# Weight passes in halves on GpSimd, all upper weight parts on ScalarE, and one-column softmax sums in a Longformer-and-MLP kernel

## The chip, the core and the metric

The kernel runs on one core of a Trainium2 chip. The core has five instruction streams: TensorE (PE, with its weight loads shown as PEld), VectorE (DVE), ScalarE (ACT), GpSimd (POOL) and SyncE (SP), which here issues all DMAs. Each engine takes its instructions strictly in the order in which they stand in its stream. The metric is the device time of one execution in microseconds, and of several runs the median. The profile is one such execution, and its lines are in microseconds unless marked ns.

## The reference

Two stages are computed one after the other. First an attention with a window and with global tokens, for 8 batches and 8 heads of width 64, with 512 local and 32 global tokens:

```python
s_g  = scale * q_g @ k_all^T            # 32 global queries see all 544 keys
s_ll = scale * q_l @ k_l^T              # 512 local queries, |i - j| <= 32 only
s_lg = scale * q_l @ k_g^T              # and the 32 global keys
out  = softmax(...) @ concat(v_g, v_l)
```

Then every token (8 x 544 = 4352 tokens of 512 features) goes through a two-layer network with 2048 hidden units and a slope per unit for negative values:

```python
h = x @ w_in
g = maximum(h, 0) + alpha * minimum(h, 0)
y = g @ w_out
```

Everything is wanted near single precision. The kernel gets there with operands that are split in two: a rounded upper part and the rest, and three matrix products of such parts in place of one.

## The kernel before, in words

**The network** is cut into 9 groups of tokens (8 batches of 512 local tokens, and one group of the 256 global tokens) and 16 blocks of 128 hidden units, so 144 steps. A step has 12 matmuls for the first layer (`f1`: `h_ps` from `xh`, `xl` and the weights `wt`), two VectorE passes for the activation (L407, L408), a rounding on ScalarE (`gh`, L410), a subtraction on GpSimd (`gl`, L411), and two steps later 12 matmuls for the second layer (`f2`: accumulated in `o`).

**The attention** goes by pairs of heads, 32 pairs of four quarter steps each, and runs ahead of the network: 19 steps (`NPRE`) of attention stand before the first network step, and later each network step carries a quarter of a pair. The first five pairs (`NRAW`) take a path with transposes on TensorE, the others go through DRAM. In each quarter step `local_scores` (L246, L250) makes two score tiles with their row minima `mn` and their row sums `z`, and the function that it returns, `softmax_tail`, adds 1e-9 to the two sums (L211), inverts them (L212) and scales the two tiles (L217 on ScalarE, or L215 on GpSimd in two quarter steps of the first pair).

**The weights** arrive in double precision, as pairs of 32-bit words, in 32 pieces of 128 x 512 (16 blocks, two layers). Each piece is turned to single precision and split in two. `decode_words` uses ScalarE twice (L113, L114), VectorE three times (L115, L117, L118, each over 128 x 512) and GpSimd once (L120, an integer addition over 128 x 512). One round later `split_weights` makes the upper part `wt[:, 0]` by a rounding copy, on VectorE for the blocks 0 to 7 (L127; `WV = range(0, 8)`, so 16 pieces) and on ScalarE for the blocks 8 to 15 (L129), and the lower part `wt[:, 1]` on GpSimd (L130). In the first 19 steps 13 pieces are decoded, later 3 pieces in two steps, until none is left; this ends while the first batch is in the network. After that only attention and network remain.

**What sets the order.** The code is written in steps, and a scheduler with a model of the engines then orders the instructions of every engine. From the 25th step on (`PIN`) TensorE's matmuls keep the order of the program; what belongs to the attention gets a higher priority from the fifth step on. Matmuls without use (`warm`, two and two in each of the first 18 steps) only keep TensorE busy.

Tiles of the names `wt`, `wr` and `g` are buffers of 128 x 512 elements in SBUF; `wt` in the first rows of a piece is the tile under work, and in L127 to L130 the final pair of parts.

Of the kernel before, what the change touches and what calls it, by code (L numbers as in the profile page):

```python
# [8 lines left out]
F32 = mybir.dt.float32  # L9
# [4 lines left out]
ALU = mybir.AluOpType  # L14
# [12 lines left out]
NWARM = 18  # L27
WARM = (2, 2)
NRAW = 5
WV = range(0, 8)  # L30
NWB = 33
NST = 18
NNP = [(0, 0), (0, 2)]
# [27 lines left out]
def longformer_ffn(ctx: ExitStack, tc: tile.TileContext, qk, qkr, gn, vt, vx, w, alpha, out):  # L61
    nc = tc.nc
# [35 lines left out]
    def stage(name, dtype=F32):  # L98
        return work.tile([128, 512], dtype, tag="st", name=name, bufs=NST)
# [9 lines left out]
    def decode_words(f, j):  # L109
        words = wraw.pop((f, j)).rearrange("p (n two) -> p n two", two=2)  # L110
        low, high = words[:, :, 0], words[:, :, 1]
        t, r = stage("wt"), stage("wr", I32)
        nc.scalar.activation(t, high.bitcast(F32), AF.Abs)  # L113
        nc.scalar.activation(r, low, AF.Copy, scale=2.0**-29)  # L114
        nc.vector.tensor_scalar(t, t, CLAMP_LO, CLAMP_HI, op0=ALU.max, op1=ALU.min)  # L115
        tu = t.bitcast(U32)
        nc.vector.tensor_scalar(tu, tu, 3, 0x3FFFFFFF, op0=ALU.logical_shift_left, op1=ALU.bitwise_and)  # L117
        nc.vector.scalar_tensor_tensor(tu, high, 0xC0000000, tu, op0=ALU.bitwise_and, op1=ALU.bitwise_or)  # L118
        ti = t.bitcast(I32)
        nc.gpsimd.tensor_tensor(ti, ti, r, op=ALU.add)  # L120
        wmid[f, j] = t

    def split_weights(f, j):
        t = wmid.pop((f, j))
        wt = wpool.tile([128, 2, 512], F32R, tag="w", name="wt")
        if f in WV:
            nc.vector.tensor_copy(wt[:, 0, :], t)  # L127
        else:
            nc.scalar.copy(wt[:, 0, :], t)  # L129
        nc.gpsimd.tensor_tensor(wt[:, 1, :], t, wt[:, 0, :].bitcast(F32), op=ALU.subtract)  # L130
        wts[f, j] = wt

    rmask = stage("rmask")[:, 0:480].rearrange("p (i n) -> p i n", i=3)
# [71 lines left out]
    def small(name, n=2):  # L205
        return work.tile([128, n], F32, tag=name, name=name, bufs=3)

    def softmax_tail(ranges, z, n, pool=False):
        parts = 128
        rz = small("rz")  # L210
        nc.vector.tensor_scalar(rz[:parts, 0:n], z[:parts, 0:n], 1e-9, None, op0=ALU.add)  # L211
        nc.vector.reciprocal(rz[:parts, 0:n], rz[:parts, 0:n])  # L212
        for e, r in enumerate(ranges):
            if pool:
                nc.gpsimd.tensor_scalar(r, r, rz[:parts, e : e + 1], 1.0, op0=ALU.mult, op1=ALU.mult)  # L215
            else:
                nc.scalar.activation(r, r, AF.Copy, scale=rz[:parts, e : e + 1])  # L217

    def local_scores(P, h, a, pool=False):
# [24 lines left out]
        for e, pr in enumerate(ranges):  # L244
# [4 lines left out]
            )  # L249
            nc.scalar.activation(pr, pr, AF.Exp, bias=mn[:, e : e + 1], scale=-1.0, accum_out=z[:, e : e + 1])  # L250
        return lambda: softmax_tail(ranges, z, 2, pool)

    gbank = {}
# [282 lines left out]
    def weights_step(u):  # L536
        k = state[0]
        n = RATE[0][u % len(RATE[0])] if u < NPRE else RATE[1][u % len(RATE[1])]
        new = [i for i in range(k, min(k + n, len(pieces)))]
        for i in new:  # L540
            if i + ahead < len(pieces):
                load_weights(*pieces[i + ahead])
            decode_words(*pieces[i])
        state[0] += len(new)
        done.append([pieces[i] for i in new])
        if len(done) > 1:
            for key in done.pop(0):
                split_weights(*key)
# [10 lines left out]
    for t in range(-NPRE, NT + LAG):  # L559
# [6 lines left out]
        G, f = divmod(t + 1, NF)  # L566
# [93 lines left out]
```

## Time and profile before

| | |
|---|---|
| median of 3 runs | 1049.59 us (1046.12 to 1050.47) |
| the profiled execution | 1047.16 us, of which the span from the first to the last instruction is 1045.4 us |
| PE busy | 989.7 us (95% of the span) |
| DVE busy | 702.2 us (67%) |
| ACT busy | 502.4 us (48%) |
| POOL busy | 429.6 us (41%) |
| mean granted TensorE clock | 0.966 of full speed |

A row of a group names the source line, the engine, the operation, the tiles with their shapes and the count; then the busy time in us and the mean duration of one in ns; then the idle time of the engine just before these instructions, with what ended it. A row of a timeline names the start in us, the duration in us, the engine, the line, the operation and the tiles. A row of a table by stages names the stretch, its length, and then for PE, PEld, DVE, ACT and POOL the busy time and in brackets the number of instructions; last come the granted TensorE clock, the share of time that the DMA engines were busy, and the GB/s that they moved. The granted clock is 1.00 at full speed and 0.50 at half.

### The profile page before, as it was taken

The numbers are of one execution on the slowest core, as the hardware profiler recorded it, in microseconds if no ns is written. First come the engines' busy times: TensorE is split into PE (matmuls) and PEld (weight loads), VectorE is DVE, ScalarE is ACT, GpSimd is POOL, SyncE is SP. The second block draws the span as 40 slices with busy tenths as digits, with TensorE's granted clock in tenths as the row PEclk, the third lists the DMA queues.
The fourth block names the chain that finished last, engine by engine and source line by source line (L and its number), as shares of the span: only waits on it lengthen the run. The fifth ranks groups of instructions, "written<-read, shape, count | busy, mean of one in ns | idle before, by whom it ended". The sixth has DMA issues, their size and how long they took to land.

```text
span 1045.4 us, 16948 instructions
## 1 busy us (share of the span) xinstructions
PE 989.7 (95%) x5466; PEld 795.0 (76%) x5466; DVE 702.2 (67%) x2189; ACT 502.4 (48%) x1337; POOL 429.6 (41%) x342
## 2 busy tenths in 40 slices
PE   7789988789999999999999999999999999999998
PEld 4455666667888878887888788878887788888798
DVE  8984999987666866676667766676667666322322
ACT  5465576655544555465455545555445443211121
POOL 6621777774333334343444344434443431122222
PEclk9985798899999999999999999999999999999999
DMA  9461266435544554455444554455445433100010
GB/s 338 177 204 67 100 208 211 138 89 166 147 142 141 156 170 140 142 163 170 140 145 142 155 159 141 139 162 154 139 141 169 152 116 90 52 1 1 1 41 21
DMA packets 103626, 139.39 MB, mean 133 GB/s; under 512 B 11056, under 2 KB 59952, under 8 KB 103536
## 3 DMA queue, kind: packets, MB, share of 16 engines
q1 hardware_dynamic: 103536, 138.30, 43.2%
q8 instruction: 43, 0.70, 0.3%
q14 instruction: 47, 0.39, 0.1%
HBM read 104.57 MB, written 33.69 MB: 132 GB/s over the span
## 4 chain that ended last, share of the span: by engine, by line
PE 73%; DVE 17%; DMA 3%; issue 3%; ACT 1%; POOL 1%; SPq 1%; DVEq 0%; ACTq 0%; POOLq 0%
PE o L93 31%; PE h_ps L93 29%; PE o_ps L93 5%; PE s_ps L93 4%; PE g_ps L93 3%; DVE wt L118 2%; DVE wt L115 2%; DMA rawq<-in_qk_dram 2%; DVE wt L117 2%; DVE p_sb L246 2%; DVE g L407 1%; DVE pt_sb L300 1%; DVE rz L211 1%; DVE g L408 1%; DMA out_dram<-ost 1%
## 5 line engine op out<-in xcount | busy, mean ns | idle before, releaser
L411 POOL TENSOR_TENSOR gl<-g,gh 128x512 fp32r<-128x512 f32 (+1 forms) x144 | 178.8, 1242 | 441.2 <-ACT gh L410 410.1
L93 PE MATMUL h_ps<-xh,wt 128*128 128x512 f32 (+1 forms) x1152 | 350.2, 387 | 6.9 <-DVE g L408 6.6
L93 PE MATMUL o<-gh,wt 128*128 128x512 f32 (+1 forms) x1152 | 282.1, 387 | 3.5 <-ACT ost L305 3.5
L93 PEld LDWEIGHTS o<-gh,wt 128*128 128x128 f32 x1152 | 204.9, 188 | 52.9 <-ACT ost L305 9.3
L93 PEld LDWEIGHTS h_ps<-xh,wt 128*128 128x128 f32 x1152 | 206.4, 191 | 46.3 <-DVE g L408 4.1
L93 PE MATMUL h_ps<-xl,wt 128*128 128x512 f32 (+1 forms) x576 | 221.6, 386 | 1.1 <-DVE xl L390 1.1
L410 ACT CAST gh<-g 128x512 fp32r<-128x512 f32 (+1 forms) x144 | 85.8, 596 | 270.7 <-DVE g L408 254.2
L407 DVE TENSOR_SCALAR g<-h_ps,alpha_sb 128x512 f32<-128x512 f32 (+1 forms) x144 | 103.1, 716 | 117.0 <-PE h_ps L93 116.1
L217 ACT ACTIVATE p_sb<-p_sb,rz 128x192 f32<-128x192 f32 (+1 forms) x252 | 102.6, 455 | 151.8 <-DVE rz L212 149.7
L93 PE MATMUL o<-gl,wt 128*128 128x512 f32 (+1 forms) x576 | 150.6, 383 | 0.3 <-POOL gl L411 0.3
L250 ACT ACTIVATE p_sb<-p_sb,mn 128x192 f32<-128x192 f32 (+2 forms) x256 | 115.9, 454 | 39.1 <-DVE mn L246 38.8
L93 PEld LDWEIGHTS h_ps<-xl,wt 128*128 128x128 f32 x576 | 109.1, 190 | 25.0 <-DVE xl L390 1.8
L93 PEld LDWEIGHTS o<-gl,wt 128*128 128x128 f32 x576 | 105.0, 188 | 24.4 <-POOL gl L411 0.7
L300 DVE STREAM_TRANSPOSE pt_sb<-sg_sb 32x64 f32<-32x64 f32 x432 | 102.0, 236 | 28.5 <-ACT sg_sb L283 21.6
L196 POOL TENSOR_TENSOR hi<-rawq,hi 64x512 fp32r<-64x512 f32 x54 | 70.6, 1307 | 121.7 <-DMA vt<-in_vt_dram 46.7
L211 DVE TENSOR_SCALAR rz<-z 128x2 f32<-128x2 f32 x128 | 54.7, 427 | 90.3 <-ACT p_sb L250 89.4
L408 DVE SCALAR_TENSOR_TENSOR g<-h_ps,g 128x512 f32<-128x512 f32 (+1 forms) x144 | 93.9, 652 | 2.8
L93 PE MATMUL o_ps<-pt_sb,vt 128*64 128x160 f32 (+4 forms) x808 | 70.4, 309 | 20.2 <-DVE mn L246 18.9
L199 POOL TENSOR_TENSOR kl<-rawk,hi 128x640 fp32r<-128x640 f32 x54 | 86.6, 1603 | 3.8
L93 PEld LDWEIGHTS o_ps<-pt_sb,vt 128*64 128x64 f32 (+2 forms) x808 | 51.9, 146 | 38.6 <-DVE mn L246 23.2
L246 DVE CUSTOM_DVE_ANT_0 p_sb<-s_ps,mask 128x192 f32<-128x192 f32 x216 | 71.9, 362 | 9.4 <-PE s_ps L93 8.2
L327 DVE STREAM_TRANSPOSE p_sb<-p_sb 128x896 f32<-128x896 f32 x54 | 59.6, 1104 | 9.0 <-ACT p_sb L217 9.0
(86 smaller groups left out, 1041.0 us busy)
## 6 DMA issues: line engine op xcount, KB each, us to landing
scratch<-p_sb SPq DMA_DIRECT2D x216, 112.0 KB, 2.3
rawk<-in_qk_dram SPq DMA_DIRECT2D x108, 160.0 KB, 3.0
wraw<-in_w_dram SPq DMA_DIRECT2D x32, 512.0 KB, 7.0
vt<-in_vt_dram SPq DMA_DIRECT2D x32, 512.0 KB, 5.1
rawq<-in_qk_dram SPq DMA_DIRECT2D x108, 128.0 KB, 2.7
pt_sb<-scratch SPq DMA_DIRECT2D x54, 256.0 KB, 2.8
pt_sb<-scratch SPq DMA_DIRECT2D x54, 192.0 KB, 2.9
gn<-in_gn_dram SPq DMA_DIRECT2D x32, 304.0 KB, 5.4
```

The lines of the kernel that those rows point to most:

```text
L93: ins = nc.tensor.matmul(*a, **k)
L196: nc.gpsimd.tensor_tensor(q, raw[64:128], q.bitcast(F32), op=ALU.subtract)
L199: nc.gpsimd.tensor_tensor(kl[P, h], raw, t.bitcast(F32), op=ALU.subtract)
L211: nc.vector.tensor_scalar(rz[:parts, 0:n], z[:parts, 0:n], 1e-9, None, op0=ALU.add)
L217: nc.scalar.activation(r, r, AF.Copy, scale=rz[:parts, e : e + 1])
L246: nc.vector.tensor_tensor_reduce(out=pr, in0=s[:, 256 * e : 256 * e + nn], in1=masks[e], scale=-0.125, scalar=3.0e38, op0=ALU.add, op1=ALU ...
L250: nc.scalar.activation(pr, pr, AF.Exp, bias=mn[:, e : e + 1], scale=-1.0, accum_out=z[:, e : e + 1])
L300: nc.vector.transpose(dst, src)
L407: nc.vector.tensor_scalar(g[:, 0:n], h[:, 0:n], 0.0, alpha_sb[:, f : f + 1], op0=ALU.min, op1=ALU.mult)
L408: nc.vector.scalar_tensor_tensor(g[:, 0:n], h[:, 0:n], 0.0, g[:, 0:n], op0=ALU.max, op1=ALU.add)
L410: nc.scalar.copy(gh[:, 0:n], g[:, 0:n])
L411: nc.gpsimd.tensor_tensor(gl[:, 0:n], g[:, 0:n], gh[:, 0:n].bitcast(F32), op=ALU.subtract)
```

## The change

Three edits are made together. GpSimd's two passes over each weight piece (the integer addition of L120 and the subtraction of L130) are each issued as two instructions of 256 columns. The rounding of the upper part goes to ScalarE for all 16 blocks, so the 16 casts on VectorE (L127) are gone and ScalarE has 16 more. In `softmax_tail` the addition of 1e-9 is issued once for each of the two columns of sums; the inversion still takes both.

```diff
-WV = range(0, 8)
...
-        nc.gpsimd.tensor_tensor(ti, ti, r, op=ALU.add)
+        for c in (0, 256):
+            cs = slice(c, c + 256)
+            nc.gpsimd.tensor_tensor(ti[:, cs], ti[:, cs], r[:, cs], op=ALU.add)
         wmid[f, j] = t
...
         t = wmid.pop((f, j))
         wt = wpool.tile([128, 2, 512], F32R, tag="w", name="wt")
-        if f in WV:
-            nc.vector.tensor_copy(wt[:, 0, :], t)
-        else:
-            nc.scalar.copy(wt[:, 0, :], t)
-        nc.gpsimd.tensor_tensor(wt[:, 1, :], t, wt[:, 0, :].bitcast(F32), op=ALU.subtract)
+        nc.scalar.copy(wt[:, 0, :], t)
+        for c in (0, 256):
+            cs = slice(c, c + 256)
+            nc.gpsimd.tensor_tensor(wt[:, 1, cs], t[:, cs], wt[:, 0, cs].bitcast(F32), op=ALU.subtract)
         wts[f, j] = wt
...
         rz = small("rz")
-        nc.vector.tensor_scalar(rz[:parts, 0:n], z[:parts, 0:n], 1e-9, None, op0=ALU.add)
+        for e in range(n):
+            nc.vector.tensor_scalar(rz[:parts, e : e + 1], z[:parts, e : e + 1], 1e-9, None, op0=ALU.add)
         nc.vector.reciprocal(rz[:parts, 0:n], rz[:parts, 0:n])
```

The scheduler orders the changed program anew. Line numbers in the changed kernel differ by one or two from those before (L118 is L117 there, L211 is L212, L129 is L127, L217 is L218, L250 is L251).

VectorE in the first quarter steps of the first pair, from the last of the three passes over the first weight piece on, before (numbers behind a name are tile numbers; `wt` with `wraw` is a piece under decoding, `rz` the sums with 1e-9, `p_sb` the score tiles):

```order
L118 SCALAR_TENSOR_TENSOR wt_165<-wraw_123,wt_165 128x512
L117 TENSOR_SCALAR wt_199<-wt_199 128x512
L211 TENSOR_SCALAR rz_150<-z_141 128x2
L246 ISA p_sb_71,mn_215<-s_ps_214,rmask_92 128x160
L246 ISA mn_215 128x1
L246 ISA p_sb_71,mn_215<-s_ps_214,rmask_92 128x160
L246 ISA mn_215 128x1
L118 SCALAR_TENSOR_TENSOR wt_199<-wraw_125,wt_199 128x512
L212 RECIPROCAL rz_150<-rz_150 128x2
L211 TENSOR_SCALAR rz_188<-z_179 128x2
L115 TENSOR_SCALAR wt_294<-wt_294 128x512
L127 CAST wt_207<-wt_165 128x512
```

The same place on VectorE in the changed program:

```order
L117 SCALAR_TENSOR_TENSOR wt_166<-wraw_123,wt_166 128x512
L212 TENSOR_SCALAR rz_150<-z_141 128x1
L116 TENSOR_SCALAR wt_202<-wt_202 128x512
L212 TENSOR_SCALAR rz_150<-z_141 128x1
L247 ISA p_sb_71,mn_220<-s_ps_219,rmask_92 128x160
L247 ISA mn_220 128x1
L247 ISA p_sb_71,mn_220<-s_ps_219,rmask_92 128x160
L247 ISA mn_220 128x1
L212 TENSOR_SCALAR rz_190<-z_181 128x1
L117 SCALAR_TENSOR_TENSOR wt_202<-wraw_125,wt_202 128x512
L213 RECIPROCAL rz_150<-rz_150 128x2
L212 TENSOR_SCALAR rz_190<-z_181 128x1
```

The two-column addition has become two one-column additions that stand apart, the second of them behind a weight pass, and the cast of the first piece is no longer in VectorE's stream.

ScalarE at the same time, before (`wt` and `wr` from `wraw` are the two reads of a piece, `p_sb` with `mn` is an exponential, `p_sb` with `rz` a scaling):

```order
L250 ACTIVATE p_sb_71,z_216<-p_sb_71,mn_215 128x160
L113 ACTIVATE wt_475<-wraw_131 128x512
L114 ACTIVATE wr_476<-wraw_131 128x512
L217 ACTIVATE p_sb_71<-p_sb_71,rz_188 128x160 x2
L250 ACTIVATE p_sb_71,z_274<-p_sb_71,mn_273 128x160 x2
L113 ACTIVATE wt_509<-wraw_133 128x512
L114 ACTIVATE wr_510<-wraw_133 128x512
L305 COPY pt_sb_72<-pt0_235 128x4x2x64
```

And in the changed program:

```order
L251 ACTIVATE p_sb_71,z_221<-p_sb_71,mn_220 128x160
L127 CAST wt_211<-wt_166 128x512
L218 ACTIVATE p_sb_71<-p_sb_71,rz_190 128x160 x2
L112 ACTIVATE wt_490<-wraw_131 128x512
L113 ACTIVATE wr_491<-wraw_131 128x512
L251 ACTIVATE p_sb_71,z_281<-p_sb_71,mn_280 128x160 x2
L127 CAST wt_271<-wt_202 128x512
L112 ACTIVATE wt_526<-wraw_133 128x512
L113 ACTIVATE wr_527<-wraw_133 128x512
L127 CAST wt_367<-wt_302 128x512
```

The casts now stand between exponentials and scalings of the attention; each reads a tile that GpSimd's addition of the same piece has finished.

## The prediction

> **What bounds the kernel now.** I read the table by stages first, then the chain of waits of each stage, then the groups and the timeline of the engine that the chain names. In the stages the columns are stretch, length, busy time of PE, PEld, DVE, ACT and POOL, the granted clock, DMA share and GB/s:
>
> ```profile
> 0.00:62.00 62.00, 48.04 (x239) 29.88 (x240) 56.39 (x150) 32.03 (x87) 40.55 (x48) 0.92 0.71 255
> 62.00:104.00 42.00, 37.62 (x274) 24.09 (x274) 24.13 (x125) 25.62 (x86) 4.25 (x3) 0.66 0.33 108
> 104.00:256.00 152.00, 129.31 (x658) 102.11 (x656) 142.49 (x357) 93.21 (x230) 104.24 (x78) 0.90 0.50 150
> 256.00:1000.00 744.00, 733.66 (x3952) 598.07 (x3951) 465.73 (x1530) 344.70 (x922) 270.27 (x201) 1.00 0.43 127
> 75.70:116.60 40.90, 36.50 (x195) 23.91 (x196) 25.71 (x97) 24.24 (x73) 10.74 (x8) 0.50 0.29 100
> ```
>
> Stage A (0 to 62 us) has the first 12 weight pieces and the attention of the first pairs; VectorE is busy for 91% of it. Stage B (62 to 104) has attention with hardly any weights; TensorE is busy for 90% at a clock of 0.66. Stage C (104 to 256) has the other 20 pieces and the first network steps; VectorE is busy for 94%, TensorE for 85%. Stage D is the rest: TensorE is busy for 98.6% until 1000 us, and 10.3 us are all that any change of the other engines could win there. The chain, for stage A and then for stage C:
>
> ```profile
> by line: DVE wt L118 12.7%; DVE wt L115 12.3%; DVE rz L211 9.1%; DMA wraw<-in_w_dram 8.2%; issue 8.1%; PE warm L93 7.8%; DVE wt L127 7.7%; DVE wt L117 7.2%; DVE p_sb L246 5.5%; PE s_ps L93 5.3%; DVE pt_sb L321 1.8%; DVE gz L280 1.4%; DVE pt
> by line: issue 11.3%; DVE wt L118 9.3%; DVE wt L115 9.1%; DVE pt_sb L300 8.2%; DVE wt L117 7.7%; DVE g L407 7.2%; DVE rz L211 5.6%; DVE p_sb L246 5.4%; DVE g L408 4.4%; DVE p_sb L327 3.6%; DVE wt L127 2.4%; DMA rawq<-in_qk_dram 2.4%; DVE xl
> ```
>
> The five VectorE lines that the change touches or that meet its GpSimd passes (L115, L117, L118, L127, L211) hold 49.0% of the chain in A and 34.1% in C. So what happens to them decides.
>
> The timeline shows why they are so long (start, duration):
>
> ```profile
> 9.70 0.68 DVE L118 SCALAR_TENSOR_TENSOR wt<-wraw,wt 128x512 uint32<-128x512 uint32 x1
> 10.30 0.42 DVE L117 TENSOR_SCALAR wt<-wt 128x512 uint32<-128x512 uint32 x1
> 10.56 1.29 POOL L120 TENSOR_TENSOR wt<-wt,wr 128x512 int32<-128x512 int32 x1 [3.63 <-ACT p_sb L250]
> 10.63 1.25 DVE L211 TENSOR_SCALAR rz<-z 128x2 f32<-128x2 f32 x1
> 12.96 0.14 DVE L211 TENSOR_SCALAR rz<-z 128x2 f32<-128x2 f32 x1
> ...
> 198.04 1.46 POOL L120 TENSOR_TENSOR wt<-wt,wr 128x512 int32<-128x512 int32 x1 [1.90 <-DVE rz L211]
> 198.41 1.65 DVE L118 SCALAR_TENSOR_TENSOR wt<-wraw,wt 128x512 uint32<-128x512 uint32 x1
> 199.46 1.72 POOL L411 TENSOR_TENSOR gl<-g,gh 128x512 fp32r<-128x512 f32 x1
> 199.98 1.49 DVE L115 TENSOR_SCALAR wt<-wt 128x512 f32<-128x512 f32 x1
> 201.14 1.47 POOL L120 TENSOR_TENSOR wt<-wt,wr 128x512 int32<-128x512 int32 x1
> ```
>
> L211, over two columns, takes 0.14 us alone and 1.25 us when a GpSimd pass has begun 0.07 us before; it ends with that pass (11.88 against 11.85). L118 takes 0.68 us alone and 1.65 us under a pass of GpSimd. So the two engines exclude each other in these forms. The last three rows show a second thing: L115 gets its turn between two GpSimd passes that follow each other directly (it ends at 201.47, 0.33 us into the second).
>
> **The change part by part.** First the prices before, the VectorE groups of stage A, then of stage C, then L127 over the whole run and a one-column operation of the same kind:
>
> ```profile
> L118 DVE SCALAR_TENSOR_TENSOR wt<-wraw,wt 128x512 uint32<-128x512 uint32 x12 | 10.9, 910 | 0.1
> L127 DVE CAST wt<-wt 128x512 fp32r<-128x512 f32 x12 | 8.3, 688 | 0.1
> L115 DVE TENSOR_SCALAR wt<-wt 128x512 f32<-128x512 f32 x12 | 8.2, 686 | 1.1 <-ACT wt L113 1.1
> L117 DVE TENSOR_SCALAR wt<-wt 128x512 uint32<-128x512 uint32 x12 | 8.1, 677 | 0.1
> L211 DVE TENSOR_SCALAR rz<-z 128x2 f32<-128x2 f32 x9 | 6.2, 694 | 0.1
> ...
> L118 DVE SCALAR_TENSOR_TENSOR wt<-wraw,wt 128x512 uint32<-128x512 uint32 x20 | 20.1, 1004 | 0.2
> L117 DVE TENSOR_SCALAR wt<-wt 128x512 uint32<-128x512 uint32 x20 | 16.1, 807 | 0.3
> L115 DVE TENSOR_SCALAR wt<-wt 128x512 f32<-128x512 f32 x20 | 15.6, 782 | 0.1
> L211 DVE TENSOR_SCALAR rz<-z 128x2 f32<-128x2 f32 x18 | 9.8, 544 | 1.5 <-ACT p_sb L250 1.4
> ...
> L127 DVE CAST wt<-wt 128x512 fp32r<-128x512 f32 x16 | 12.1, 758 | 0.1
> L274 DVE TENSOR_SCALAR gm<-gm 128x1 f32<-128x1 f32 x32 | 4.8, 150 | 0.7
> ```
>
> *The casts.* All 16 leave VectorE: 8.3 us in A, 12.1 - 8.3 = 3.8 us in C. On ScalarE they cost 16 x 0.612 = 9.8 us (row L129 below). ScalarE is busy for 32.0 of 62 us in A and 93.2 of 152 in C, so they fit into its idle time; what they may hold up is a rival below.
>
> *The sums.* L274 has the same operation over one column; its mean over all 32 is 0.150 us, against 0.694 and 0.544 for L211 in A and C, so a one-column operation isn't held up. Two in place of one cost 0.30 us: A saves 6.2 - 18 x 0.15 = 3.5 us, C saves 9.8 - 36 x 0.15 = 4.4 us. If the second one only costs the spacing of two short operations, less than 0.15, it is up to 2 us more.
>
> A rule of the Trainium skill speaks against this part: VectorE: DVE Perf Modes, "Rules for kernel authors", asks to keep the number of chained VectorE operations small, since each pays its own fixed time. By it alone the split adds 27 x 0.15 = 4.0 us to the two stages in place of the saving; the L211 rows at 10.63 and 12.96 speak for the saving.
>
> *The halves.* GpSimd's groups: L120 and L130 in A, all passes with two inputs in C, and one operation at both widths:
>
> ```profile
> L120 POOL TENSOR_TENSOR wt<-wt,wr 128x512 int32<-128x512 int32 x12 | 17.0, 1418 | 12.5 <-ACT p_sb L250 3.6 <-DVE wt L118 3.4 <-DVE gm L276 1.7
> L130 POOL TENSOR_TENSOR wt<-wt 128x512 fp32r<-128x512 f32 x12 | 16.3, 1359 | 7.7 <-DVE wt L127 6.2 <-DVE rz L211 1.2 <-DVE rz L212 0.4
> ...
> L130 POOL TENSOR_TENSOR wt<-wt 128x512 fp32r<-128x512 f32 x20 | 27.2, 1364 | 2.0 <-DVE wt L127 1.4 <-ACT wt L129 0.5
> L120 POOL TENSOR_TENSOR wt<-wt,wr 128x512 int32<-128x512 int32 x20 | 26.4, 1321 | 19.6 <-DVE wt L118 10.4 <-DVE g_ps L259 3.3 <-DVE rz L211 1.9
> L411 POOL TENSOR_TENSOR gl<-g,gh 128x512 fp32r<-128x512 f32 x18 | 24.6, 1369 | 19.3 <-ACT gh L410 19.3
> L199 POOL TENSOR_TENSOR kl<-rawk,hi 128x640 fp32r<-128x640 f32 x9 | 15.3, 1702 | 0.2
> L196 POOL TENSOR_TENSOR hi<-rawq,hi 64x512 fp32r<-64x512 f32 x9 | 12.4, 1382 | 20.5 <-ACT hi L193 16.1 <-issue 3.3 <-POOL gl L411 0.7
> ...
> L411 POOL TENSOR_TENSOR gl<-g,gh 128x512 fp32r<-128x512 f32 x128 | 167.0, 1305 | 404.0 <-ACT gh L410 378.8 <-issue 25.2
> L411 POOL TENSOR_TENSOR gl<-g,gh 128x256 fp32r<-128x256 f32 x16 | 11.8, 738 | 37.2 <-ACT gh L410 31.3 <-issue 5.9
> ```
>
> Two halves take 2 x 0.738 = 1.476 us against 1.305, 13% more GpSimd time. The time that VectorE's three weight lines now lose, at 0.42, 0.42 and 0.68 us alone: in A 27.2 - 12 x 1.52 = 9.0 us; in C 51.8 - 20 x 1.52 = 21.4 us, of which the weight passes hold 53.6 of 105.9 us of GpSimd's time, so 10.8 us. An operation that falls into a pass waits for half of it on average: 0.37 in place of 0.65 us, in 13% more cases, so 36% less: 3.2 us in A and 3.9 us in C. The lower bound is zero (VectorE isn't let in between the halves), the upper one 43%. The halves of L130 also start later than a cast on VectorE would let them, since the cast is 0.61 us on ScalarE against 0.41; in A, where the network has hardly begun, nothing waits for a weight piece that closely.
>
> *On the path.* A saves 8.3 + 3.5 + 3.2 = 15.0 us of VectorE's time, C 3.8 + 4.4 + 3.9 = 12.1 us. Of the time of the five lines the chain now carries 49.0% of 62 = 30.4 us against 41.7 us busy, 73%, and 34.1% of 152 = 51.8 against 65.5 us, 79%. With these shares A gives 11.0 us and C 9.6 us. The next bounds aren't reached: in A GpSimd starts its weights at 10.56 us and needs 24 x 1.476 = 35.4 us for them, so 46 against 51 us; in C TensorE's 129 us stand against 142. B gives nothing: TensorE carries it. In D the one-column sums free VectorE too, but PE's waits there are few:
>
> ```profile
> PE o_ps L93 <- DVE mn L246: 7.8, 5, 1.6
> L129 ACT CAST wt<-wt 128x512 fp32r<-128x512 f32 x16 | 9.8, 612 | 1.2 <-POOL wt L120 1.2
> ```
>
> I put down 1 us for D (bounds 0 and 3), and take off 2 us for waits that go over to ScalarE and GpSimd. The sum is 11.0 + 9.6 + 1 - 2 = 19.6 us, against the profiled execution 1047.2 - 19.6 = 1027.6 us. The median before lies 2.4 us above that execution; I add half of this and forecast **1029 us**. With the shares at one half and nothing for the halves it is 9.5 us of gain; with all of VectorE's saving on the path and 3 us in D it is 30.
>
> **The rivals.**
>
> *GpSimd becomes the bound, or keeps its turn between two halves.* For it: in A its 46 us come close to the new length, and in the new order it has runs of four and six halves. Against it: L115 at 199.98 got in. Price: 3.2 x 0.73 + 3.9 x 0.79 = 5.4 us, and 3 us more where GpSimd's end sets the end of A: gain 11, 1037 us. The rule on the number of operations would end in the same place: 7.9 us of saving and 4.0 us of added time at 0.76 make 9 us less, 1038 us.
>
> *TensorE's clock.* The last row of the stages has half speed for 40.9 us while PE is busy for 36.5. If the earlier attention keeps the clock up there, half of 36.5 us falls away at most, bounded by VectorE's 25.7 us busy to 15 us: gain 27 to 35, about 1015 us. The Trainium skill, TensorE: Matmul & The Clock Gate, Part 1, lets the full clock return after one busy window of about 3.4 us; by this rule the stretch shouldn't last as it does, and this case would be the likelier one. The trace disagrees, 89% busy at half speed, so I keep the stretch.
>
> *VectorE's time isn't what counts.* What is freed turns into other waits (the 8.1% and 11.3% "issue" of the chains, the DMA for `rawq`), and at most a quarter arrives: gain 0 to 5, about 1045 us. Against it speak the shares of 91% and 94%.
>
> *Slower: ScalarE stands still at the casts.* In the new order a cast stands in front of scalings and exponentials of the attention, and waits for both halves of its piece's addition; ScalarE takes nothing past it. If each of the 16 waits for a pair of halves (1.48 us), 16 x 1.48 x 0.73 = 17 us come back and the gain is nearly gone. It is slower from 1.7 us per cast; with two pairs ahead of each, 2.95 us, it is 34 us against 20, 1061 us. For it: in the new order the additions of three pieces, six halves, stand ahead of the first subtraction. Against it: the 16 casts that ScalarE has now waited for 1.2 us in all.
>
> **How the numbers follow.** Forecast 0.57, with its own range 1020 to 1036; GpSimd as bound or the turn kept 0.10; the rule on the number of operations 0.03; clock 0.12; VectorE not counting 0.10; ScalarE standing still 0.08. The range of 1012 to 1046 leaves out most of the slower case and the far end of the clock's. Of this kernel a difference of 0.5% (5.2 us) can be told from none. Faster by more has the forecast, the two cases at 1037 and the clock: 0.82; within 0.5% 0.10; slower 0.08.
>
> **What would show it.** In the new profile, no cast of `wt` on VectorE; the sums at about 0.15 us each with none above 0.3; the weight passes on GpSimd at about 0.74 us; L115 and L117 nearer to 0.6 and L118 nearer to 0.85 us; stage A's last weight subtraction some 11 us earlier; the start of the unbroken run of network steps near 235 in place of 256 us; from there on the same length. The forecast is wrong if VectorE's three weight lines keep their means (the halves don't work), if ScalarE shows waits for GpSimd of several us, if the half-speed stretch is much shorter or longer than 41 us, or if the later stage differs by more than 3 us.

## The result, and the profile after

The changed kernel takes **1021.48 us** (median of 4 runs, 1020.95 to 1021.83), against 1048.59 us for the kernel before beside it (4 runs, 1046.12 to 1050.47): a ratio of 0.9744, 95% interval 0.9722 to 0.9766. The profiled execution took 1020.95 us, with a span of 1019.2 against 1045.4, so 26.2 us less. One of the four runs of e6_halves_casts below, 1344 us at a mean granted clock of 0.66 where all other runs have 0.96 to 0.99, is left out of its figures.

The line numbers shift a little: L115 is now L114, L117 is L116, L118 is L117, L120 is L121, L129 is L127, L211 is L212, L246 is L247, L407 is L408; L130 stays. For the reckoning I cut both spans at the same event, the twentieth network activation, where the unbroken run of network steps begins. In the timelines of VectorE (start, duration) it is, before and after:

```profile
264.29 0.75 DVE L407 TENSOR_SCALAR g<-h_ps,alpha_sb 128x512 f32<-128x512 f32 x1
```

```profile
249.04 0.75 DVE L408 TENSOR_SCALAR g<-h_ps,alpha_sb 128x512 f32<-128x512 f32 x1
```

So the stretch up to it, which the prediction cut into A, B and C, is 15.3 us shorter. The run behind it, D, is taken up to the last activation. The table by stretches (stretch, length, busy time of PE, PEld, DVE, ACT and POOL, granted clock, DMA share, GB/s), before:

```profile
0.00:264.30 264.30, 223.28 (x1204) 162.50 (x1206) 226.97 (x639) 156.27 (x415) 153.55 (x131) 0.86 0.53 170
264.30:1037.00 772.70, 762.36 (x4233) 628.65 (x4230) 473.60 (x1549) 345.03 (x919) 275.35 (x210) 1.00 0.41 122
```

and after:

```profile
0.00:249.00 249.00, 212.30 (x1204) 155.34 (x1205) 202.29 (x661) 164.32 (x431) 169.94 (x195) 0.91 0.56 179
249.00:1010.70 761.70, 760.80 (x4235) 630.61 (x4230) 465.71 (x1637) 345.52 (x919) 275.30 (x210) 1.00 0.41 124
```

Three things are to be seen. D, which the prediction left alone but for 1 us, is 11.0 us shorter, and PE's idle time in it has gone from 10.3 to 0.9 us. In the first stretch VectorE has 24.7 us less to do, near the 27.1 that the prediction worked out, but only 15.3 arrive. And GpSimd has 16.4 us more to do there.

The groups of the first stretch after the change (count, busy us, mean ns; then idle time of the engine before them and its releasers):

```profile
L130 POOL TENSOR_TENSOR wt<-wt 128x256 fp32r<-128x256 f32 x64 | 53.5, 858 | 7.2 <-ACT wt L127 7.1
L121 POOL TENSOR_TENSOR wt<-wt,wr 128x256 int32<-128x256 int32 x64 | 51.5, 827 | 11.9 <-ACT p_sb L251 3.7 <-DVE wt L117 2.3 <-DVE gm L277 1.1
L117 DVE SCALAR_TENSOR_TENSOR wt<-wraw,wt 128x512 uint32<-128x512 uint32 x32 | 30.7, 960 | 0.3
L114 DVE TENSOR_SCALAR wt<-wt 128x512 f32<-128x512 f32 x32 | 24.2, 757 | 5.2 <-ACT wt L112 5.1
L116 DVE TENSOR_SCALAR wt<-wt 128x512 uint32<-128x512 uint32 x32 | 23.4, 732 | 0.3
L127 ACT CAST wt<-wt 128x512 fp32r<-128x512 f32 x32 | 19.8, 618 | 0.5 <-POOL wt L121 0.5
L212 DVE TENSOR_SCALAR rz<-z 128x1 f32<-128x1 f32 x78 | 10.6, 146 | 7.4 <-ACT p_sb L251 6.9
```

The sums are as short as forecast. The half passes take 0.83 to 0.86 us, not 0.74, and the three weight lines of VectorE keep their means (before 0.746, 0.758 and 0.969 us). A stretch of the timelines of both engines shows what became of the halves:

```profile
23.51 0.93 DVE L117 SCALAR_TENSOR_TENSOR wt<-wraw,wt 128x512 uint32<-128x512 uint32 x1
23.86 2.06 POOL L121 TENSOR_TENSOR wt<-wt,wr 128x256 int32<-128x256 int32 x2
24.36 0.96 DVE L114 TENSOR_SCALAR wt<-wt 128x512 f32<-128x512 f32 x1
25.36 0.84 DVE L116 TENSOR_SCALAR wt<-wt 128x512 uint32<-128x512 uint32 x1
```

The two engines take turns: VectorE does get in between two halves, two halves then take 2.06 us, where those in the row at 54.72 us further down take 1.42, and VectorE's 0.42 us operations still take 0.84 to 0.96.

Where did D's 11 us come from? At the same place in both programs, behind the start of a batch, the timeline before has

```profile
479.53 1.57 POOL L199 TENSOR_TENSOR kl<-rawk,hi 128x640 fp32r<-128x640 f32 x1
479.59 1.54 DVE L211 TENSOR_SCALAR rz<-z 128x2 f32<-128x2 f32 x1 [2.29 <-ACT p_sb L250]
481.42 0.83 ACT L217 ACTIVATE p_sb<-p_sb,rz 128x224 f32<-128x224 f32 x2 [1.36 <-DVE rz L212]
482.29 1.11 DVE L327 STREAM_TRANSPOSE p_sb<-p_sb 128x896 f32<-128x896 f32 x1 [0.96 <-ACT p_sb L217]
484.02 1.21 PE L93 MATMUL o_ps<-pt_sb,vt 128*64 128x160 f32 x16 [1.57 <-DVE mn L246]
```

and after

```profile
461.15 1.57 POOL L199 TENSOR_TENSOR kl<-rawk,hi 128x640 fp32r<-128x640 f32 x1
461.20 0.15 DVE L212 TENSOR_SCALAR rz<-z 128x1 f32<-128x1 f32 x1 [0.28 <-ACT p_sb L251]
464.25 1.70 PE L92 MATMUL o_ps<-pt_sb,vt 128*64 128x160 f32 x24
```

Before, the two-column sum began 0.06 us after the pass over the attention's keys (L199) and was held for its whole length. The scaling on ScalarE and the transposition on VectorE came later by that, and behind them on VectorE the score reductions (`mn`), for which PE stood still for 1.57 us. PE's five gaps of 1.55 to 1.58 us in D all lie like this, each ending some 4.4 us after such a held sum has begun (369.34, 479.59, 589.85, 700.10 and 810.37 us). After, the one-column sum runs under the same pass in 0.15 us, and the gaps are gone. These five gaps are 7.8 of the 11.0 us. PE's waits in D beside them, first a line from before, then the only one that is left after the change:

```profile
PE o L93 <- ACT ost L305: 1.6, 5, 0.3
PE h_ps L92 <- DVE xl L391: 0.9, 1, 0.9
```

The five short waits for `ost` went with the sums too, but weren't followed back, and the last 1.6 us are in PE's busy time, whose ends are modelled.

### The profile page after: what moved, and what is told of

Its sections match the earlier page's. It is cut to its first block, busy times and chain, and to the rows that moved or that the text cites. A ratio compares the mean times of both kernels' runs of the same rounds, so it can differ in the third digit from the quotient of the medians.

```text
span 1019.2 us, 17170 instructions
## 1 busy us (share of the span) xinstructions
PE 977.2 (96%) x5466; PEld 789.9 (78%) x5466; DVE 669.7 (66%) x2301; ACT 510.9 (50%) x1353; POOL 446.0 (44%) x406
## 4 chain that ended last, share of the span: by engine, by line
PE 83%; DVE 8%; DMA 4%; issue 2%; ACT 2%; POOL 1%; SPq 0%; DVEq 0%; ACTq 0%; POOLq 0%
PE o L92 35%; PE h_ps L92 35%; PE o_ps L92 5%; PE s_ps L92 5%; PE g_ps L92 3%; DMA wraw<-in_w_dram 2%; DVE wt L117 1%; DVE wt L114 1%; DVE g L408 1%; DVE pt_sb L301 1%; DVE p_sb L247 1%; DVE g L409 1%; DMA rawq<-in_qk_dram 1%; DVE wt L116 1%; DMA pt_sb<-scratch 0%
## 5 line engine op out<-in xcount | busy, mean ns | idle before, releaser
L408 DVE TENSOR_SCALAR g<-h_ps,alpha_sb 128x512 f32<-128x512 f32 (+1 forms) x144 | 103.3, 717 | 128.5 <-PE h_ps L92 127.4
L218 ACT ACTIVATE p_sb<-p_sb,rz 128x192 f32<-128x192 f32 (+1 forms) x252 | 102.5, 456 | 121.1 <-DVE rz L213 120.9
L251 ACT ACTIVATE p_sb<-p_sb,mn 128x192 f32<-128x192 f32 (+2 forms) x256 | 116.3, 456 | 32.5 <-DVE mn L247 32.0
L212 DVE TENSOR_SCALAR rz<-z 128x1 f32<-128x1 f32 x256 | 37.9, 151 | 96.6 <-ACT p_sb L251 95.3
L199 POOL TENSOR_TENSOR kl<-rawk,hi 128x640 fp32r<-128x640 f32 x54 | 85.7, 1586 | 3.8
L247 DVE CUSTOM_DVE_ANT_0 p_sb<-s_ps,mask 128x192 f32<-128x192 f32 x216 | 72.0, 363 | 12.9 <-PE s_ps L92 10.7
L92 PE MATMUL o_ps<-pt_sb,vt 128*64 128x160 f32 (+4 forms) x808 | 68.3, 300 | 8.6 <-DVE mn L247 4.4
```

The source lines that it names most:

```text
L92: ins = nc.tensor.matmul(*a, **k)
L199: nc.gpsimd.tensor_tensor(kl[P, h], raw, t.bitcast(F32), op=ALU.subtract)
L247: nc.vector.tensor_tensor_reduce(out=pr, in0=s[:, 256 * e : 256 * e + nn], in1=masks[e], scale=-0.125, scalar=3.0e38, op0=ALU.add, op1=ALU ...
L408: nc.vector.tensor_scalar(g[:, 0:n], h[:, 0:n], 0.0, alpha_sb[:, f : f + 1], op0=ALU.min, op1=ALU.mult)
```

## The experiments

The kernels ran in four groups, each beside runs of the kernel before on the same chip: e1 to e4 (median before 1046.89 us, 16 runs), e5 to e7 (1047.40, 7), e9 to e11 (1047.11, 13), e12 and e13 (1046.47, 7). Ratios are to these. A scheduler makes the order of the program from the operations' costs, so each kernel has an order of its own; where this matters it is said. The stretches are cut as above, up to the twentieth activation and from there to the last.

**The sums alone (e1_sums).**

```diff
-        nc.vector.tensor_scalar(rz[:parts, 0:n], z[:parts, 0:n], 1e-9, None, op0=ALU.add)
+        for e in range(n):
+            nc.vector.tensor_scalar(rz[:parts, e : e + 1], z[:parts, e : e + 1], 1e-9, None, op0=ALU.add)
```

> One part alone: the 1e-9 sums as one-column operations, casts and GpSimd passes as before. By the prediction's terms (3.5 x 0.73 + 4.4 x 0.79 + 1 in the stage from the start of the unbroken network run) it gains 7 us: about 1040 us. The rival, formed from the two traces: in the later stage each batch's two-column sum was held by the GpSimd pass L199 and PE stood still behind it, so the sums give 11 us there (steps of 2 to 2.5 us at the batch starts) and up to 6 before it: 1030 to 1036 us. If the 11 us came from the shifted order of the program and not from the sums, the later stage keeps its length and the time stays at 1041 or above.

1030.93 us (4 runs, 1028.17 to 1033.30), ratio 0.9838, interval 0.9801 to 0.9875: 16.0 us faster, more than twice the 7 that the prediction's terms give. Its stretches:

```profile
0.00:260.60 260.60, 225.03 (x1204) 163.26 (x1206) 224.93 (x677) 156.51 (x415) 153.66 (x131) 0.86 0.53 171
260.60:1021.90 761.30, 760.41 (x4233) 630.22 (x4230) 465.64 (x1638) 345.46 (x919) 275.01 (x210) 1.00 0.41 124
```

D has 761.3 us in place of 772.7: the sums bring all of D's gain by themselves, and 3.7 us ahead of it.

**The casts alone (e2_casts).**

```diff
-WV = range(0, 8)
+WV = range(0, 0)
```

> One part alone: all 32 casts on ACT, two-column sums and whole GpSimd passes as before. The prediction's terms (8.3 x 0.73 + 3.8 x 0.79) give 9 us, all before the unbroken network run: about 1038 us, later stage unchanged within 1 us. The rival: what the first 62 us gained of 10 us is the casts' alone, and the half-clock stretch shortens with them (another 5 us): 1032 us. If ACT stands still behind GpSimd at the casts the time is 1047 or more.

1040.64 us (7 runs, 1038.38 to 1043.02), ratio 0.9932, interval 0.9908 to 0.9956: 6.2 us faster.

```profile
0.00:258.90 258.90, 216.82 (x1204) 159.01 (x1206) 217.91 (x622) 164.79 (x431) 152.24 (x131) 0.89 0.55 173
258.90:1031.60 772.70, 762.38 (x4233) 628.62 (x4230) 474.92 (x1548) 344.93 (x919) 275.27 (x210) 1.00 0.41 122
```

All of it lies in the first stretch (5.4 us in the profiled execution); D isn't touched. That is two thirds of the predicted 9.1.

**The halves alone (e3_halves).** The two passes of GpSimd over a weight piece (L120, L130) as in the change, nothing else.

> One part alone: GpSimd's weight passes in halves, the rest as before. The prediction's term is 3.2 x 0.73 + 3.9 x 0.79 = 5 us of gain: 1042 us, with the three weight lines on DVE at 0.6, 0.6 and 0.85 us. The rival, from the trace after the change (0.9 us per half in the first stage, weight lines as long as before): no gain or a loss, GpSimd taking 24 x (2 x 0.9 - 1.39) = 10 us more in the first stage of which DVE's casts leave some hidden: 1047 to 1057 us.

1043.56 us (10 runs, 1040.41 to 1043.98), ratio 0.9959, interval 0.9939 to 0.9979: 3.3 us faster, nearer to the first expectation. D took 773.0 us, unchanged.

**Casts and sums, whole passes (e4_casts_sums).** The change without its halves.

> The change without its halves: casts on ACT and one-column sums, whole GpSimd passes. By the prediction's terms the halves carry 5.4 us, so this is slower than the whole change: about 1027 us. The rival: the halves gave nothing (DVE's weight lines kept their means and GpSimd spent 0.9 us per half in place of 0.7), so this takes as long as the whole change or less: 1010 to 1021 us.

1021.88 us (4 runs, 1018.37 to 1024.79), ratio 0.9751, interval 0.9712 to 0.9790: the same as the whole change. Its stretches, and its groups in the first:

```profile
0.00:249.20 249.20, 211.25 (x1206) 154.50 (x1208) 214.44 (x662) 163.70 (x431) 151.80 (x131) 0.92 0.56 179
249.20:1010.80 761.60, 760.70 (x4233) 630.50 (x4228) 465.61 (x1638) 345.46 (x919) 274.99 (x210) 1.00 0.41 124
```

```profile
L130 POOL TENSOR_TENSOR wt<-wt 128x512 fp32r<-128x512 f32 x32 | 44.1, 1382 | 5.3 <-ACT wt L129 5.3
L120 POOL TENSOR_TENSOR wt<-wt,wr 128x512 int32<-128x512 int32 x32 | 42.9, 1342 | 31.6 <-DVE wt L118 11.8 <-ACT p_sb L251 4.2 <-DVE rz L213 3.9
L117 DVE TENSOR_SCALAR wt<-wt 128x512 uint32<-128x512 uint32 x32 | 30.5, 954 | 0.2
L118 DVE SCALAR_TENSOR_TENSOR wt<-wraw,wt 128x512 uint32<-128x512 uint32 x32 | 29.6, 925 | 0.3
L115 DVE TENSOR_SCALAR wt<-wt 128x512 f32<-128x512 f32 x32 | 24.6, 770 | 3.2 <-ACT wt L113 3.0
```

This is the right neighbour for judging the halves, not the kernel before. With whole passes the three weight lines take 84.7 us, with halves 78.3: 6.4 us less on VectorE, near the forecast 7.1. GpSimd pays 105.0 against 87.0 us for it, 21% more, where 13% was forecast. The first stretch ends at 249.0 or 249.2 us either way. So the halves do what they were forecast to do on VectorE, and once casts and sums are there they bring nothing that can be told from none.

**Halves and sums without the casts (e5_halves_sums), halves and casts without the sums (e6_halves_casts).**

> The change without the casts on ACT: halves and one-column sums, casts of 16 pieces still on DVE. The prediction's terms: 1029 + 9 = 1038 us. From the traces, if the sums give the later stage's 11 us by themselves and the casts the first stage's 10: 1021 + 10 = 1031 us. If the order of the program rather than the casts made the first stage shorter: about 1021 us.

> The change without the one-column sums: halves and casts, two-column sums as before. The prediction's terms: 7 us slower than its forecast, 1036 us, later stage as long as in the whole change to 1 us. The rival: without the one-column sums the later stage is 11 us longer again, with PE waiting at the batch starts, and the early stages lose up to 6: 1032 to 1038 us, of which 11 us after the start of the unbroken network run.

e5_halves_sums: 1029.05 us (4 runs, 1024.86 to 1029.28), ratio 0.9809, interval 0.9774 to 0.9844, with D at 761.3 us and the first stretch at 257.6: the casts are worth 7.6 us on top of the other two. e6_halves_casts: ratio 0.9921, interval 0.9891 to 0.9952 (3 runs, 1038.48 to 1040.95), so 17 us or more are lost without the sums. Between e2_casts and e6_halves_casts (ratios 0.9932 and 0.9921) the halves show no gain that can be told from none, nor beside the sums alone (e5_halves_sums 0.9809, e1_sums 0.9838, with intervals that overlap).

**No addition at all (e7_casts_noadd).** e4_casts_sums with the addition of 1e-9 left out, so that its operations' own time shows.

```diff
-        nc.vector.tensor_scalar(rz[:parts, 0:n], z[:parts, 0:n], 1e-9, None, op0=ALU.add)
-        nc.vector.reciprocal(rz[:parts, 0:n], rz[:parts, 0:n])
+        nc.vector.reciprocal(rz[:parts, 0:n], z[:parts, 0:n])
```

> Casts on ACT, whole GpSimd passes, and the addition of 1e-9 left out altogether (the reciprocal takes z itself; z is at least 1, since the largest score contributes exp(0), and 1 + 1e-9 rounds to 1 in fp32). If what counted in the sums is only that they no longer wait for GpSimd, this equals casts plus one-column sums to 2 us. If the one-column operations themselves cost time on the path (256 x 0.15 = 38 us of DVE, a sixth of it before the network run), it is 3 to 6 us faster. If the reciprocal over two columns takes over the wait for GpSimd, the later stage is 11 us longer again: 1030 us or more.

1022.43 us (4 runs, 1020.28 to 1024.45), ratio 0.9758, interval 0.9730 to 0.9786, D at 761.6: as with the one-column sums. These sums' own 38 us of VectorE cost nothing that shows in the time, and the reciprocal over two columns isn't held in their place:

```profile
L211 DVE RECIPROCAL rz<-z 128x2 f32<-128x2 f32 x128 | 21.0, 164 | 67.4 <-ACT p_sb L249 66.3
```

**Two columns again, with the same number of operations (e9_wide_again).** The question left was whether the form of the sum counts, or the order that the scheduler made of twice as many operations. On e4_casts_sums, in place of the loop:

```diff
+        nc.vector.tensor_scalar(rz[:parts, 0:1], z[:parts, 0:1], 1e-9, None, op0=ALU.add)
+        nc.vector.tensor_scalar(rz[:parts, 0:n], z[:parts, 0:n], 1e-9, None, op0=ALU.add)
```

> Casts on ACT, whole GpSimd passes, and as many sum operations as in the change, but the second of each pair covers both columns again (it repeats the first column). PE's order is that of e4_casts_sums but for some rows. If the one-column form counts because a two-column sum is held by GpSimd's passes: the later stage's 11 us come back (steps of 2.3 us at the batch starts) and the 6 to 9 us before it too, 1021.9 + 17 to 20 = 1039 to 1042 us, like casts alone (1040.6). If the order that the program took is what counts, it stays within 3 us of 1021.9.

1037.79 us (10 runs, 1036.67 to 1046.12), ratio 0.9922, interval 0.9896 to 0.9948: 15.9 us are back. PE's order differs from that of e4_casts_sums in a few rows only, yet D has its old length, with five waits of PE for `mn` again, 6.4 us in all. (The profiled execution took 1045.55 us, 7.8 above the median, so its first stretch isn't that of a median run.)

```profile
263.20:1035.40 772.20, 762.25 (x4231) 628.54 (x4228) 483.00 (x1637) 345.24 (x919) 275.48 (x210) 1.00 0.41 122
```

And one stretch of its timeline holds both forms, each begun under a GpSimd pass:

```profile
21.03 1.47 POOL L130 TENSOR_TENSOR wt<-wt 128x512 fp32r<-128x512 f32 x1
21.28 0.14 DVE L211 TENSOR_SCALAR rz<-z 128x1 f32<-128x1 f32 x1
23.59 1.28 POOL L120 TENSOR_TENSOR wt<-wt,wr 128x512 int32<-128x512 int32 x1 [1.09 <-DVE wt L118]
23.72 1.17 DVE L212 TENSOR_SCALAR rz<-z 128x2 f32<-128x2 f32 x1
```

So D's gain comes from the form of the addition and not from the order: with the second column it is held, with one it isn't.

**VectorE's cast time given back (e11_spare_cast).** On e4_casts_sums, ACT's casts kept:

```diff
             nc.scalar.copy(wt[:, 0, :], t)
+        if f < 8:
+            nc.vector.tensor_copy(wt[:, 1, :], t)
```

> e4_casts_sums, and for the first 16 pieces DVE makes a cast more, into the lower half that GpSimd then overwrites: ACT's casts stay, DVE gets its 16 x 0.75 = 12 us back. If the casts' gain is DVE's time alone, all that the casts gave beside the sums comes back: 1021.9 + 9 = 1031 us, the time of the sums alone. If the gain came from the order that the program took, or from ACT's doing it, less than 4 us come back.

1035.85 us (4 runs, 1030.78 to 1036.22), ratio 0.9876, interval 0.9840 to 0.9912: 14.0 us lost, with D unchanged at 761.3 and the first stretch at 264.1. Work put back on VectorE in the first stretch thus costs time, and more than the casts had brought. Two things beside VectorE's time may be in it: GpSimd's subtraction overwrites the copy and waited 3.8 us for it in all, and the scheduler's order differs throughout from that of e4_casts_sums. How much of the 14.0 us is which stays open.

**One column, two tensors (e10_global, e12_after_global).** In the softmax of the global rows L276 and L280 combine two tensors of 64x1.

```diff
-        nc.vector.tensor_tensor(m[0:64, 1:2], m[0:64, 1:2], m[0:64, 0:1], op=ALU.min)
+        nc.vector.tensor_scalar(m[0:64, 1:2], m[0:64, 1:2], m[0:64, 0:1], None, op0=ALU.min)
...
-        nc.vector.scalar_tensor_tensor(z[0:64, 1:2], z[0:64, 1:2], 1e-9, z[0:64, 0:1], op0=ALU.add, op1=ALU.add)
+        nc.vector.tensor_scalar(z[0:64, 1:2], z[0:64, 1:2], 1e-9, z[0:64, 0:1], op0=ALU.add, op1=ALU.add)
```

> e4_casts_sums, and in the softmax of the global rows the two operations with two tensors of one column each (L276 and L280, 0.4 us on average against 0.15 alone) written with the second tensor as the scalar operand. If it is the second tensor that makes a one-column operation wait for GpSimd, both go to 0.15 us; they lost 2.5 + 1.1 us before the unbroken network run, of which three quarters are on the path: 1019 to 1020 us. If the operations stay at 0.4 us, the time is 1022 and the form doesn't matter.

> The whole change, and L277 and L281 of the global softmax with the second tensor as the scalar operand, as in e10_global. If halves and whole passes are worth the same, this equals e10_global (1020.8) within 2 us. If the halves spare some of DVE's waiting that the added GpSimd time had covered, it is 2 to 4 us faster, 1017 to 1019.

The groups of the first stretch in e4_casts_sums:

```profile
L277 DVE TENSOR_TENSOR gm<-gm 64x1 f32<-64x1 f32 x9 | 4.9, 540 | 0.1
L281 DVE SCALAR_TENSOR_TENSOR gz<-gz 64x1 f32<-64x1 f32 x9 | 4.7, 520 | 0.1
```

and in e10_global:

```profile
L277 DVE TENSOR_SCALAR gm<-gm 64x1 f32<-64x1 f32 x9 | 1.8, 202 | 0.2
L281 DVE TENSOR_SCALAR gz<-gz 64x1 f32<-64x1 f32 x9 | 1.8, 201 | 0.2
```

The second tensor was what made them wait. In time e10_global is 1020.84 us (4 runs, 1019.87 to 1021.65), ratio 0.9744, interval 0.9715 to 0.9772, not to be told from e4_casts_sums. With the whole change (e12_after_global) it is 1017.86 us (4 runs, 1015.74 to 1019.41), ratio 0.9722, interval 0.9690 to 0.9755: the lowest time of this study. That is 3.0 us below e10_global, as its second expectation had it, so the halves may be worth 2 to 3 us here; but the intervals of e12_after_global, e10_global and the change overlap, and it isn't shown.

**TensorE's clock (e13_warm).** On the whole change, `NWARM = 30` in place of 18.

> The whole change, with the idle matmuls that keep TensorE's clock up put into 12 more steps (30 in place of 18), 48 matmuls of some 0.23 us. If half speed costs what the runs of the kernel before say (about 0.3 us for each us at half speed), the 46 us of it before the unbroken run fall to some 25 and 6 us are won, against up to 11 us of PE time in a stage where PE is idle for about 20: 1016 to 1024. If the clock only follows the stalls and costs nothing itself, the added matmuls cost 3 to 11 us: 1024 to 1032.

1020.24 us (4 runs, 1019.09 to 1021.28), ratio 0.9752, interval 0.9725 to 0.9779, no different from the change. The mean clock of its runs rose from 0.9775 to 0.984, so that, as 2 x (1 - clock) x span, some 32 us ran at half speed in place of 46. Net, the added matmuls cost nothing; whether half speed has a price that they ate up isn't settled by it.

## Why the prediction was right, and where it was wrong

The forecast was 1029 us with a range of 1012 to 1046; 1021.5 is inside, and the 26.2 us of the profiled executions stand against a sum of 19.6. It is right on the side, and made up differently: 15.3 us ahead of the unbroken run, where 11.0 + 9.6 - 2 = 18.6 stood, and 11.0 behind it, where 1 stood. Without the 10 us in D that it didn't foresee, the time would be some 1031 us, inside the range still, so the side and the range aren't luck. That the total comes as near as it does is in part: too little ahead and far more behind. Of the four signs that the prediction named against itself three came: the weight lines kept their means, the long stretch at half speed is much shorter, and D differs by more than 3 us. (Its lower end, 9.5 us, is 10.0 + 1 - 2 = 9.0 by its own terms, which changes nothing here.)

*Stage D, the step that failed.* "1 us for D (bounds 0 and 3)", because "PE's waits there are few". The price of the waits was in the rows that the prediction itself used: PE idle for 10.3 us, and 7.8 us of it in five waits for `mn` (L246). What was not done was to follow one of these waits back. It ends at L211 under L199, once in each of five batches. The rows of e1_sums, e4_casts_sums and e9_wide_again show it: 761.3 and 761.6 us with one-column sums, 772.2 with two columns in nearly the same PE order. Of the 90 sums in D 10 took 1.5 us, all under L199, and 5 of these stand ahead of PE's gaps: a mean over the group shows none of that.

*The sums in A and C.* Forecast 2.6 + 3.5 us on the path; alone they gave 3.7 in the first stretch. That each takes 0.15 us and isn't held came true (146 ns over 78). The Trainium skill, SBUF — State Buffer, "Who interferes with whom", says that an operation with one SBUF input outside the two-port modes doesn't contend with GpSimd, and one with two SBUF inputs does. The 64x1 rows of e10_global agree with it. By the Trainium skill, VectorE: DVE Perf Modes, "What auto-detection actually checks", an operation with one source enters a two-port mode where source and destination lie in SBUF and the outermost dimension longer than one is even in both, or equal. Two columns meet that; one column has no such dimension, a case that the page doesn't name. The rows of e9_wide_again agree with that reading, 1.17 against 0.14 us. The rule on the number of operations, which the prediction gave 0.03, finds no support in e7_casts_noadd: without the additions nothing is faster.

*The casts.* Forecast 9.1, measured 6.2 alone, 7.6 beside sums and halves (e5_halves_sums against the change), 9.1 beside the sums (e1_sums against e4_casts_sums). The order of size was right. There is no cast of `wt` on VectorE, and ScalarE shows no waits for GpSimd of several us: the 32 casts waited for 0.5 us in all (the L127 row), so the slower rival is out. The casts can be late all the same: PE's longest wait between 95.5 and 249 us after the change is for one of them, which had stood behind a scaling on ScalarE:

```profile
PE h_ps L92 <- ACT wt L127: 5.2, 1, 5.2
```

*The halves.* Forecast 5.4 us on the path; they gave 3.3 alone, and nothing that shows beside the rest (1021.88 without, 1021.48 with). The criterion that the prediction set, the weight lines' means, did fail, and yet it misleads: against the right neighbour VectorE lost 6.4 us of waiting. What failed is the multiplication by VectorE's share of the chain: 12.2 us less of its time (214.44 against 202.29) moved the first stretch by 0.2 us. This pair doesn't show why. GpSimd has 18 us more at the same time, the order is another (PE's wait of 5.2 us for a cast isn't there in e4_casts_sums), and e11_spare_cast lost time by work on VectorE, so it can't be said that VectorE no longer counts. The chain after the change in the first 56 us begins with the weights' DMA, up to 25.6 us, and VectorE's three weight lines carry 14% of it, where they had 32% of stage A before:

```profile
by line: DMA wraw<-in_w_dram 42.6%; DVE wt L117 7.0%; PE warm L92 7.0%; issue 5.2%; PE s_ps L92 4.6%; DVE wt L114 4.5%; DVE pt_sb L322 3.1%; PE h_ps L92 2.8%; DVE wt L116 2.4%; ACT wt L112 2.0%; ACT wr L113 2.0%; ACT wt L127 1.8%; DVE p_sb 
```

The rival "GpSimd becomes the bound, or keeps its turn" was right in that the halves bring little or nothing. Its second half is refuted (L114 at 24.36 got in), and that GpSimd is the bound wasn't shown: in e4_casts_sums it has 18 us less to do, and the time is the same. Which engine does bound the first stretch now stays open.

*The marks in the trace.* Stage A's last weight subtraction ends 7.0 us earlier, not 11:

```profile
61.80 1.30 POOL L130 TENSOR_TENSOR wt<-wt 128x512 fp32r<-128x512 f32 x1 [1.16 <-DVE rz L211]
```

```profile
54.72 1.42 POOL L130 TENSOR_TENSOR wt<-wt 128x256 fp32r<-128x256 f32 x2 [1.47 <-ACT wt L127]
```

The unbroken run starts 15.3 us earlier, where the marks 235 and 256 meant 21.

*The clock.* The long stretch at half speed shrank from 40.9 us to 13.7 (80.5 to 94.2 us), as its rival had it, and the total of 1015 us that the rival gave wasn't reached. e4_casts_sums has the same end of the first stretch as the change (249.2) with whole passes, and e7_casts_noadd nearly so (249.9) with a clock of 0.89 against 0.91 there. Over the four runs of e7_casts_noadd, 2 x (1 - clock) x span gives 64 us at half speed, as many as the 63 us of the kernel before (mean of 43 runs), and its ratio is 0.9758 where the change has 0.9744. So a better clock isn't a condition of the gain.

## What to carry to other kernels

When PE is nearly saturated, the few waits that it still has are the whole of what can be won there; follow each of them back to its first late instruction before giving them a price, since a small operation that is held at the same place in every round can carry them all. Beside a busy GpSimd, write VectorE's small operations in a form with one column and one tensor (the second as the scalar operand); one column in place of two alone brought 16.0 us here, the casts alone 6.2 and the halves alone 3.3. And don't expect gains to add: the halves gave 3.3 us alone and none that shows beside the rest, so measure each part beside the others, not only against the kernel before.

## What the hardware showed beside that

*Which operations are held.* Not held by GpSimd's passes are the reciprocal over two columns (0.164 us on average over 128 in e7_casts_noadd), the one-column sums, and the second half of the network's activation (L408), over 128x512, which has one of its two tensors in PSUM. From the timeline of the kernel before:

```profile
114.98 1.47 POOL L130 TENSOR_TENSOR wt<-wt 128x512 fp32r<-128x512 f32 x1
115.23 0.68 DVE L408 SCALAR_TENSOR_TENSOR g<-h_ps,g 128x512 f32<-128x512 f32 x1
115.83 0.90 DVE L117 TENSOR_SCALAR wt<-wt 128x512 uint32<-128x512 uint32 x1
```

L408 takes its mean of 0.68 us under the pass; L117, from SBUF, is held.

*The clock.* Within one kernel the time goes with it: of 43 runs of the kernel before, the 9 with a mean clock of 0.974 and more took 1043.4 us on average, the 12 with 0.9665 and less 1050.0. As time at half speed, that is about 0.31 us for each us (correlation 0.95); it is no proof of which causes which. By that price the 17 us less at half speed after the change would be 5 us of its gain, an estimate; e7_casts_noadd, with the gain and without those 17 us, speaks against it. The kernel before in windows of 3.41 us:

```profile
72.28:75.69 3.41, 1.41 (x10) 0.85 (x6) 2.91 (x16) 2.33 (x11) 0.00 (x0) 1.00 0.45 157
75.69:79.10 3.41, 3.09 (x21) 2.06 (x21) 0.96 (x7) 2.23 (x7) 0.00 (x0) 0.50 0.02 5
79.10:82.52 3.42, 3.42 (x20) 2.01 (x21) 0.71 (x5) 0.90 (x4) 0.00 (x0) 0.50 0.00 0
82.52:85.93 3.41, 3.41 (x33) 2.34 (x34) 1.27 (x6) 2.50 (x8) 0.00 (x0) 0.50 0.00 0
85.93:89.34 3.41, 2.86 (x13) 1.76 (x13) 3.30 (x11) 1.81 (x4) 2.29 (x2) 0.50 0.65 231
```

Here the clock falls to half behind a window in which PE is busy for 1.41 of 3.41 us. The Trainium skill, TensorE: Matmul & The Clock Gate, Part 1, gives it back after one busy window of about 3.4 us. The length agrees: the stretch at half speed, 75.70 to 116.60 us, is twelve such windows long. That one is enough doesn't hold here, since after two windows that PE fills (79.10 to 85.93) the next one is at half speed still. PE's ends are modelled, so how busy it was in them isn't certain.
